# Splitting the weights ahead of the third q and k: another form of the shift, another order, and four or three pieces a slot

## The chip, the cores and the metric

The kernel runs on one core of one Trainium2 chip. The time is the device time of one execution in microseconds; before the change it is 1643.41 us, the median of three runs (1642.69 to 1644.14). The core has a matrix engine (TensorE, PE in the profile; PEld are its weight loads), a vector engine (VectorE, DVE), a scalar engine (ScalarE, ACT) and GpSimd (POOL). SyncE (SP) issues the transfers. Each engine works through its own list of instructions in order.

## The reference

Attention for 8 batches of 8 heads, 576 rows of 64, where each row keeps only its 32 largest scores; then a feed-forward block with a quick GELU over the 4608 rows of 512.

```python
scores = scale * np.matmul(q, k.transpose(0, 1, 3, 2))
kth = np.partition(scores, -top_k, axis=-1)[..., -top_k:-top_k + 1]
scores = np.where(scores >= kth, scores, -1000000000.0)
scores = scores - np.max(scores, axis=-1, keepdims=True)
attn = np.exp(scores)
attn = attn / (np.sum(attn, axis=-1, keepdims=True) + 1e-09)
attn_out = np.matmul(attn, v)
...
x = attn_out.transpose(0, 2, 1, 3).reshape(B * S, H * D)
h = x @ w_in
g = h * (1.0 / (1.0 + np.exp(-1.702 * h)))
out = g @ w_out
```

q, k and v are float32. The two weight matrices (512 x 2048 and 2048 x 512) come as 64-bit floats, since a float32 array is multiplied there by a 64-bit scalar.

## The kernel before

**Slots.** The attention is cut into slots. A slot takes one block of 128 rows of two heads (a head pair `hp`, four of them per batch) against all 576 keys; the last 64 rows of two head pairs share a slot. A batch has 18 slots. The function `slot(n)` writes out by hand the order of all engines' instructions for slots -1 to 9; `two_slots` does so for the rest, two at a time. The scheduler keeps this order, so an instruction that has to wait holds up what stands behind it on its engine.

**A slot's attention.** `scores(n + 2)` multiplies q and k on TensorE (L230) and ScalarE copies the result (`sc`, L237). `topk(n)` is VectorE's work: 14 instructions, eight that find the next eight maxima (L246) for one of the two heads and six that remove them (L249), numbered i = 0 to 13. In the next slot, `bounds` turns the smallest kept value and the largest into two numbers on GpSimd (`cut`, L265, and `low`, L266); `exponentials` does two passes on ScalarE (L274, L276) and sums up; `divide`, called at i = 5 of that slot's `topk`, takes the reciprocal on VectorE (L285, L287) and makes two diagonal matrices on GpSimd (`by`, L291). `turn` multiplies by them on TensorE, `values` multiplies by v.

**Loading and preparing.** The table `later`, filled by `at(n, ...)`, says in which slot what is loaded. q and k of the first and second head pair are loaded in slot -1, of the third in slot 0, of the fourth in slot 1. `prepare` transposes them on TensorE (L198, L204), and ScalarE copies them back (L200 to L207). All transfers go through SyncE in the order in which they are written.

**Weights.** They are cut into 32 pieces of 128 x 512, 512 KB each as they are loaded, and each is turned into 32-bit numbers of a kind of the kernel's own in these steps (`round_piece`), named as in the code: *size* on ScalarE (L144, from the high word), *shift* on VectorE (L145, three bits to the left), *low* and *sign* on ScalarE (L150, L149, in place in the raw buffer) and *finish* on GpSimd, an addition and a product (L140, L141). Raw pieces lie in 8 buffers, which come free with *finish*. The list `by_slot` says how many pieces are split in which slot: 2, 3, 4, 4, 4, 4, 3, 4 and 4 in slots 0 to 8. A slot's pieces are loaded one slot ahead; their shifts stand between VectorE's instructions of `topk` after i = 7, 8 and so on, one at each; their *finish* runs in the slot after, the first at i = 2 and the others after `divide`.

The shift is a scalar_tensor_tensor with a column of zeros, `none`, as its second input, spread over 512 columns.

**The feed-forward block** starts when 128 rows of all four head pairs are there, in slot 4 for the first time: `hidden` (L378), `tanh` (L395) on ScalarE, `gate` (L411) on VectorE up to slot 9, `project` (L426) from slot 7 on.

Of the kernel before, what the change touches and what calls it, by code (L numbers as in the profile page):

```python
# [9 lines left out]
ALU = mybir.AluOpType  # L10
ENG = mybir.EngineType
F32 = mybir.dt.float32
U32 = mybir.dt.uint32
# [3 lines left out]
P = 128  # L17
# [11 lines left out]
def kernel(  # L29
# [24 lines left out]
    nc = tc.nc  # L54
# [13 lines left out]
    PIECE = 512  # L68
# [12 lines left out]
    const = ctx.enter_context(tc.tile_pool(name="const", bufs=1))  # L81
# [20 lines left out]

    ident = const.tile([P, P], F32, name="ident")
    make_identity(nc, ident[:])
    none = const.tile([P, 1], U32, name="none")
    nc.vector.memset(none[:], 0)
    win = const.tile([P, CC, DFF], F32, name="win")
    wout = const.tile([P, FC, C], F32, name="wout")

# [14 lines left out]
    def round_piece(n):  # L124

        c, g = pieces[n]
        dst = wout[:, g, :] if c is None else win[:, c, g * PIECE : (g + 1) * PIECE]
        words = raw.pop(n)[:].rearrange("p (n w) -> p n w", w=2)
        low, high = words[:, :, 0], words[:, :, 1].bitcast(F32)
        bits, whole = dst.bitcast(U32), dst.bitcast(I32)

        def finish():
            nc.gpsimd.tensor_tensor(out=whole, in0=whole, in1=low.bitcast(I32), op=ALU.add)  # L140
            nc.gpsimd.tensor_tensor(out=dst, in0=dst, in1=high, op=ALU.mult)  # L141

        return {
            "size": lambda: nc.scalar.activation(dst, high, AF.Abs, scale=REBASE),  # L144
            "shift": lambda: nc.vector.scalar_tensor_tensor(  # L145
                out=bits, in0=bits, scalar=3, in1=none[:].to_broadcast([P, PIECE]),
                op0=ALU.logical_shift_left, op1=ALU.bitwise_or,
            ),
            "sign": lambda: nc.scalar.activation(high, high, AF.Sign),  # L149
            "low": lambda: nc.scalar.mul(out=low.bitcast(I32), in_=low, mul=2.0**-29),  # L150
            "finish": finish,
        }
# [37 lines left out]
    def prepare(name, b, hp):  # L190
        src = loaded.pop((name, b, hp))


        before = 0 if name == "q" else TAIL
        dst = qkt.tile([P, S + before], F32, name=f"{name}_t")
        full = ps_t.tile([P, 512], F32, name="tp")
        for t in range(NF):
            nc.tensor.transpose(full[:, t * P : (t + 1) * P], src[:, t, :, :], ident[:])  # L198
        scale = SCALE if name == "q" else 1.0
        nc.scalar.mul(out=dst[:, before : before + FULL], in_=full[:], mul=scale)  # L200
        (qT if name == "q" else kT)[b, hp] = dst
        if name == "k":
            ends = ps_t.tile([P, 512], F32, name="tp")
            nc.tensor.transpose(ends[:, 0:P], loaded.pop(("ends", b, hp))[:], ident[:])  # L204
            nc.scalar.mul(out=qT[b, hp][:, FULL:S], in_=ends[:, 0:TAIL], mul=SCALE)
            for to in (0, before + FULL):
                nc.scalar.copy(out=dst[:, to : to + TAIL], in_=ends[:, TAIL:P])  # L207
# [12 lines left out]
    def scores(n):  # L220
        b, t, hps = slots[n]
        ps = [ps_s.tile([P, 2, 512], F32, name="s_ps") for _ in range(2)]
        if t < NF:
            parts = [(i, 0, slice(0, P), slice(t * P, (t + 1) * P)) for i in range(2)]
        else:
            parts = [(i, p, slice(p * TAIL, (p + 1) * TAIL), slice(FULL, S)) for i, p in ((0, 0), (1, 1), (0, 1), (1, 0))]
        for c in range(2):
            for i, p, rows, cols in parts:
                on = slice(i * D, (i + 1) * D)
                nc.tensor.matmul(  # L230
                    ps[i][rows, c, 0:HALF],
                    lhsT=qT[b, hps[p]][on, cols],
                    rhs=kT[b, hps[p]][on, FIRST[i] + c * HALF : FIRST[i] + (c + 1) * HALF],
                )
        sc = st[n]["sc"] = scp.tile([P, 2, S], F32, name="sc")
        for i in range(2):
            nc.scalar.copy(out=sc[:, i, :].rearrange("p (c k) -> p c k", c=2), in_=ps[i][:, :, 0:HALF])  # L237
# [22 lines left out]
    def bounds(n):  # L260

        top = st[n]["top"]
        cut = st[n]["cut"] = small.tile([P, 2], F32, name="cut")
        low = st[n]["low"] = small.tile([P, 2], F32, name="low")
        nc.gpsimd.tensor_scalar(cut[:], top[:, :, TOPK - 1], -1.0, None, op0=ALU.mult)  # L265
        nc.gpsimd.tensor_tensor(out=low[:], in0=top[:, :, TOPK - 1], in1=top[:, :, 0], op=ALU.subtract)  # L266

    def exponentials(n):

        sc, cut, low = st[n]["sc"], st[n]["cut"], st[n]["low"]  # L270
        pr = st[n]["pr"] = prp.tile([P, 2 * S], F32, name="pr")
        den = st[n]["den"] = small.tile([P, 2], F32, name="den")
        for i in range(2):
            nc.scalar.activation(sc[:, i, :], sc[:, i, :], AF.Prelu, bias=cut[:, i : i + 1], alpha=HUGE)  # L274
        for i in range(2):
            nc.scalar.activation(  # L276
                pr[:, i * S : (i + 1) * S], sc[:, i, :], AF.Exp, bias=low[:, i : i + 1],
                accum_out=den[:, i : i + 1],
            )
# [37 lines left out]
    def turn_main(n):  # L317
        for i in range(2):
            turn(n, i * NF, MAIN[i], NF)

    def turn_ends(n):

        turn(n, 2 * NF, FULL, 1)
# [114 lines left out]
    def at(n, fn, *args):  # L438
        later.setdefault(n, []).append((fn, args))
# [4 lines left out]
    READY = (((-9, -8), (-7, -6), (-4, -3), (-2, -1)), ((-7, -6), (-4, -3), (-3, -2), (-1, -2)))  # L444
    FETCH = (((-13, -12), (-11, -10), (-7, -7), (-5, -4)), ((-11, -10), (-9, -8), (-5, -5), (-2, -2)))
    VALUES = ((-8, -7, 0, 0), (-8, -7, 2, 2))
    by_slot = dict(enumerate([2, 3, 4, 4, 4, 4, 3, 4, 4]))
    for n in by_slot:
        first = sum(map(len, list(by_slot.values())[:n]))
        by_slot[n] = list(range(first, first + by_slot[n]))  # L450
# [1 line left out]
    for hp in range(NP):  # L452
        for name in "qk":
            at(max(hp - 2, -1), load, name, 0, hp)
            at(max(hp - 2, -1), prepare, name, 0, hp)
    for hp in range(NP):
        at(hp - 1, load_v, 0, hp)
    for n in by_slot:
        for x in by_slot[n]:
            at(n - 1, load_piece, x)  # L460
    for b in range(1, B):
        for hp in range(NP):
# [3 lines left out]
            at(b * PER + VALUES[b % 2][hp], load_v, b, hp)  # L466
    unfinished = []

    def slot(n):
        todo = later.pop(n, [])  # L470
        for fn, args in todo:
            if fn is not prepare:
                fn(*args)
        preparing = [args for fn, args in todo if fn is prepare]
        settled = n > PROJECTS
        aside = SETTLED < n < N
        before = 0 <= n - 1 < N
        if before:
            bounds(n - 1)
            exponentials(n - 1)  # L480
        if n < 0:
            for m in range(2):
                for args in preparing:
                    if args[2] == m:
                        prepare(*args)
                scores(m)
        some = [round_piece(x) for x in by_slot.get(n, [])]
        for piece in some:
            piece["size"]()
        if 0 <= n and not settled:  # L490
            for args in preparing:
                prepare(*args)
            scores(n + 2)
        shifts = [piece["shift"] for piece in some]
        tanh(aside)
        for i, op in enumerate(topk(n) if 0 <= n < N else [lambda: None] * 14):
            op()
            if i == 2 and unfinished:
                unfinished.pop(0)()
            if i == 5:  # L500
                if before:
                    divide(n - 1)
                while unfinished:
                    unfinished.pop(0)()
            if i == 8 and not aside:
                gate(aside)
            if i > 6 and shifts:
                shifts.pop(0)()
        if aside:
            gate(aside)  # L510
        if settled:
            for args in preparing[:1]:
                prepare(*args)
        for piece in some[:2]:
            piece["low"]()
        going = settled and len(to_project) > (2 if n < N else 0)
        if going:
            project(range(G - 1))
        if before:
            turn_main(n - 1)  # L520
        if going:
            project(range(G - 1, G))
        if before:
            turn_ends(n - 1)
        for piece in some[2:]:
            piece["low"]()
        if before:
            values(n - 1)
        for piece in some:
            piece["sign"]()  # L530
            unfinished.append(piece["finish"])
        if settled and n + 2 < N:
            scores(n + 2)
        if settled:
            for args in preparing[1:]:
                prepare(*args)
        hidden()
# [106 lines left out]
```

## Time and profile before

| | value |
|---|---|
| time, median of 3 runs | 1643.41 us |
| profiled span | 1642.3 us |
| TensorE busy | 1578.7 us, 96% |
| VectorE busy | 1497.8 us, 91% |
| ScalarE busy | 1155.6 us, 70% |
| GpSimd busy | 756.2 us, 46% |
| TensorE in the first 130 us | 81.80 us |
| VectorE in the first 130 us | 113.69 us |

The slots are told apart by VectorE's first maximum over a fresh score tile (L246, `top<-sc`):

| slot | starts at, us | length, us | pieces split | pieces finished |
|---|---|---|---|---|
| 0 | 10.71 | 10.86 | 2 | 0 |
| 1 | 21.57 | 17.22 | 3 | 2 |
| 2 | 38.79 | 16.31 | 4 | 3 |
| 3 | 55.10 | 14.71 | 4 | 4 |
| 4 | 69.81 | 14.70 | 4 | 4 |
| 5 | 84.51 | 15.97 | 4 | 4 |
| 6 | 100.48 | 14.95 | 3 | 4 |
| 7 | 115.43 | 15.55 | 4 | 3 |
| 8 | 130.98 | 15.99 | 4 | 4 |
| 9 | 146.97 | 10.50 | 0 | 4 |

Shares of busy time over the whole span mix two stages, the first some 150 us, in which the weights are split, and the rest; they have to be read apart. In a timeline row the first number is the start and the second the duration[...]. A row with "x2" holds two instructions.

### The profile page before, as it was taken

What the parts mean: (1) busy time and instruction counts of PE and PEld (TensorE: products, weight loads), DVE (VectorE), ACT (ScalarE), POOL (GpSimd) and SP (SyncE); (2) the same over time, 40 slices, a digit from 0 to 9 for tenths busy, and PEclk for the clock granted to TensorE, in tenths of its full rate; (3) what the DMA queues carried; (4) which work ended last, traced back from release to release, by engine and by line L of the source; (5) the groups of instructions that cost most, each with busy time, mean ns of one, the idle gap of its engine ahead of it and who ended that gap; (6) DMA issues with size and microseconds to landing.
All of it is one profiled execution on the core that took longest, in us unless ns stands there. A gap on an engine that the chain in (4) does not pass through costs nothing.

```text
span 1642.3 us, 31956 instructions
## 1 busy us (share of the span) xinstructions
PE 1578.7 (96%) x11923; PEld 1179.0 (72%) x11923; DVE 1497.8 (91%) x3212; ACT 1155.6 (70%) x2449; POOL 756.2 (46%) x783
## 2 busy tenths in 40 slices
PE   5478899999999999999999999999999999999999
PEld 4466677777777777777777777777777777777776
DVE  6999999999999999999999998999999999999960
ACT  5886677777777777777777777677777777777761
POOL 2787444444444444444444444444444444444430
PEclk7789999999999999999999999999999999999999
DMA  8342101110001001101000100111000100000000
GB/s 215 116 142 62 29 22 29 29 43 16 22 15 43 22 22 29 30 22 37 8 21 9 43 22 22 30 29 44 15 22 15 43 22 22 22 8 8 7 8 14
DMA packets 125723, 56.59 MB, mean 34 GB/s; under 512 B 116864, under 2 KB 116864, under 8 KB 125568
## 3 DMA queue, kind: packets, MB, share of 16 engines
q1 hardware_dynamic: 125568, 54.55, 12.6%
q8 instruction: 94, 1.54, 0.4%
q14 instruction: 61, 0.50, 0.1%
HBM read 45.09 MB, written 9.44 MB: 33 GB/s over the span
## 4 chain that ended last, share of the span: by engine, by line
PE 88%; DVE 8%; ACT 2%; POOL 1%; issue 1%; DMA 0%; SPq 0%; POOLq 0%; ACTq 0%
PE ph L378 30%; PE po L426 29%; PE s_ps L230 10%; PE o L337 9%; PE tp L305 8%; DVE top L246 3%; DVE left L249 2%; PE tp L198 2%; DVE wout L145 1%; DVE win L145 1%; ACT sc L237 1%; DMA k_l<-in_k_dram 0%; ACT pr L276 0%; PE tp L204 0%; POOL wout L141 0%
## 5 line engine op out<-in xcount | busy, mean ns | idle before, releaser
L246 DVE MAX8 top<-left 128x8 f32<-128x576 f32 x864 | 610.1, 746 | 0.0
L426 PE MATMUL po<-wout,gT 128*128 128x512 f32 x1152 | 541.3, 593 | 0.0
L378 PEld LDWEIGHTS ph<-xT,win 128*128 128x128 f32 x4096 | 468.1, 192 | 41.8 <-issue 41.0
L378 PE MATMUL ph<-xT,win 128*128 128x128 f32 x4096 | 485.1, 277 | 0.0
L249 DVE MATCH_REPLACE8 left<-top,left 128x576 f32<-128x576 f32 x576 | 423.4, 742 | 0.0
L294 POOL TENSOR_SCALAR pr<-pr,rden 128x576 f32<-128x576 f32 x135 | 232.9, 1725 | 358.9 <-ACT th L395 354.9
L408 POOL TENSOR_SCALAR th<-th 128x512 f32<-128x512 f32 x133 | 198.7, 1494 | 224.2 <-ACT th L395 220.8
L274 ACT ACTIVATE sc<-sc,cut 128x576 f32<-128x576 f32 x288 | 208.1, 774 | 132.0 <-POOL cut L265 132.0
L315 ACT COPY pt<-tp 128x512 f32<-128x512 f32 (+1 forms) x432 | 193.2, 480 | 153.0 <-PE tp L305 142.5
L426 PEld LDWEIGHTS po<-wout,gT 128*128 128x128 f32 x1152 | 197.6, 191 | 142.0 <-issue 141.8
L237 ACT COPY sc<-s_ps 128x576 f32<-128x576 f32 x288 | 169.8, 643 | 78.4 <-PE s_ps L230 78.1
L305 PEld LDWEIGHTS tp<-ident,pr 128*128 128x128 f32 x1215 | 145.5, 141 | 108.7 <-issue 59.3
L276 ACT ACTIVATE pr<-sc,low 128x576 f32<-128x576 f32 x288 | 219.1, 764 | 0.0
L249 DVE MATCH_REPLACE8 left<-top,sc 128x576 f32<-128x576 f32 x288 | 211.5, 742 | 0.0
L246 DVE MAX8 top<-sc 128x8 f32<-128x576 f32 x288 | 201.9, 742 | 9.9 <-ACT sc L237 9.9
L230 PE MATMUL s_ps<-k_t,q_t 64*128 64x288 f32 (+1 forms) x1280 | 183.4, 433 | 1.3 <-ACT k_t L200 1.3
L305 PE MATMUL tp<-ident,pr 128*128 128x128 f32 x1215 | 177.2, 273 | 5.0 <-ACT pt L315 4.0
L409 POOL TENSOR_TENSOR gT<-th,h 128x512 f32<-128x512 f32 x133 | 169.6, 1275 | 11.1
L337 PE MATMUL o<-pt,v_l 128*64 128x128 f32 (+1 forms) x2560 | 160.8, 269 | 1.4 <-ACT pt L315 0.6
L337 PEld LDWEIGHTS o<-pt,v_l 128*64 128x64 f32 x2560 | 133.5, 139 | 31.6 <-ACT pt L315 16.1
L230 PEld LDWEIGHTS s_ps<-k_t,q_t 64*128 64x128 f32 (+1 forms) x1280 | 100.2, 178 | 60.2 <-issue 40.9
L265 POOL TENSOR_SCALAR cut<-top 128x2 f32<-128x2 f32 x144 | 32.2, 224 | 221.4 <-DVE top L246 217.3
(51 smaller groups left out, 1186.6 us busy)
## 6 DMA issues: line engine op xcount, KB each, us to landing
q_l<-in_q_dram SPq DMA_DIRECT2D x64, 128.0 KB, 2.6
k_l<-in_k_dram SPq DMA_DIRECT2D x64, 128.0 KB, 2.7
v_l<-in_v_dram SPq DMA_DIRECT2D x64, 128.0 KB, 2.6
raw<-in_moe_w_in_dram SPq DMA_DIRECT2D x16, 512.0 KB, 4.5
raw<-in_moe_w_out_dram SPq DMA_DIRECT2D x16, 512.0 KB, 3.6
out_dram<-ob SPq DMA_DIRECT2D x32, 256.0 KB, 2.1
ends<-in_q_dram SPq DMA_DIRECT2D x32, 32.0 KB, 2.3
ends<-in_k_dram SPq DMA_DIRECT2D x32, 32.0 KB, 2.4
```

Source lines behind the costliest of these rows:

```text
L230: nc.tensor.matmul(ps[i][rows, c, 0:HALF], lhsT=qT[b, hps[p]][on, cols], rhs=kT[b, hps[p]][on, FIRST[i] + c * HALF : FIRST[i] + (c + 1) * ...
L246: nc.vector.max(top[:, i, 8 * r : 8 * r + 8], (left if r else sc)[:, i, :])
L249: nc.vector.match_replace(left[:, i, :], top[:, i, 8 * r : 8 * r + 8], (left if r else sc)[:, i, :], LOWEST)
L274: nc.scalar.activation(sc[:, i, :], sc[:, i, :], AF.Prelu, bias=cut[:, i : i + 1], alpha=HUGE)
L276: nc.scalar.activation(pr[:, i * S : (i + 1) * S], sc[:, i, :], AF.Exp, bias=low[:, i : i + 1], accum_out=den[:, i : i + 1],)
L294: nc.gpsimd.tensor_scalar(pr[:, S : 2 * S], pr[:, S : 2 * S], rden[:, 1:2], None, op0=ALU.mult)
L305: nc.tensor.transpose(tp[:, c * P : (c + 1) * P], pr[:, at], ident[:])
L315: nc.scalar.copy(out=to, in_=tp[:, 0 : blocks * P])
L337: nc.tensor.matmul(o[j * D : (j + 1) * D, 0 : cols.stop - cols.start], lhsT=main[:, c, j, :] if c < NF else tail[:, j, :], rhs=pt[:, j * N ...
L378: nc.tensor.matmul(ph[:, i, :], lhsT=win[:, c, f * P : (f + 1) * P], rhs=xT[:, c, :], start=(c == 0), stop=(c == CC - 1),)
L408: nc.gpsimd.tensor_scalar(th[:], th[:], 1.0, None, op0=ALU.add)
L426: nc.tensor.matmul(po[:], lhsT=gT[:, i, :], rhs=wout[:, f, :], start=(f == 0), stop=(f == FC - 1))
```

## The change

Three things are changed. The shift becomes a tensor_scalar with one input, and the tile of zeros goes. Of slot 0's pieces the first two are loaded in slot -1 right after the first q and k; their *size* steps stand on ScalarE right after the copy of slot 0's scores, their *low* and *sign* at the start of slot 0, and their shifts at i = 1 and 2 of slot 0's `topk`. And the pieces are dealt out as 4, 3, 3, 4, 3, 4, 3, 4, 4. In slot 0, the preparation of the third q and k and the scores of slot 2 are written behind `topk`, after the *size* steps of pieces 2 and 3, whose shifts stand at i = 12 and 13. The purpose is to take work from VectorE in the opening stage and to use the start, when GpSimd has no pieces yet. What is computed stays the same.

```diff
--- before.py
+++ after.py
@@ -102,8 +102,6 @@
 
     ident = const.tile([P, P], F32, name="ident")
     make_identity(nc, ident[:])
-    none = const.tile([P, 1], U32, name="none")
-    nc.vector.memset(none[:], 0)
     win = const.tile([P, CC, DFF], F32, name="win")
     wout = const.tile([P, FC, C], F32, name="wout")
 
@@ -142,10 +140,7 @@
 
         return {
             "size": lambda: nc.scalar.activation(dst, high, AF.Abs, scale=REBASE),
-            "shift": lambda: nc.vector.scalar_tensor_tensor(
-                out=bits, in0=bits, scalar=3, in1=none[:].to_broadcast([P, PIECE]),
-                op0=ALU.logical_shift_left, op1=ALU.bitwise_or,
-            ),
+            "shift": lambda: nc.vector.tensor_scalar(bits, bits, 3, None, op0=ALU.logical_shift_left),
             "sign": lambda: nc.scalar.activation(high, high, AF.Sign),
             "low": lambda: nc.scalar.mul(out=low.bitcast(I32), in_=low, mul=2.0**-29),
             "finish": finish,
@@ -444,7 +439,7 @@
     READY = (((-9, -8), (-7, -6), (-4, -3), (-2, -1)), ((-7, -6), (-4, -3), (-3, -2), (-1, -2)))
     FETCH = (((-13, -12), (-11, -10), (-7, -7), (-5, -4)), ((-11, -10), (-9, -8), (-5, -5), (-2, -2)))
     VALUES = ((-8, -7, 0, 0), (-8, -7, 2, 2))
-    by_slot = dict(enumerate([2, 3, 4, 4, 4, 4, 3, 4, 4]))
+    by_slot = dict(enumerate([4, 3, 3, 4, 3, 4, 3, 4, 4]))
     for n in by_slot:
         first = sum(map(len, list(by_slot.values())[:n]))
         by_slot[n] = list(range(first, first + by_slot[n]))
@@ -453,10 +448,13 @@
         for name in "qk":
             at(max(hp - 2, -1), load, name, 0, hp)
             at(max(hp - 2, -1), prepare, name, 0, hp)
+        if hp == 0:
+            for x in by_slot[0][:2]:
+                at(-1, load_piece, x)
     for hp in range(NP):
         at(hp - 1, load_v, 0, hp)
     for n in by_slot:
-        for x in by_slot[n]:
+        for x in by_slot[n][0 if n else 2 :]:
             at(n - 1, load_piece, x)
     for b in range(1, B):
         for hp in range(NP):
@@ -466,7 +464,10 @@
             at(b * PER + VALUES[b % 2][hp], load_v, b, hp)
     unfinished = []
 
+    early = []
+
     def slot(n):
+        nonlocal early
         todo = later.pop(n, [])
         for fn, args in todo:
             if fn is not prepare:
@@ -484,13 +485,22 @@
                     if args[2] == m:
                         prepare(*args)
                 scores(m)
-        some = [round_piece(x) for x in by_slot.get(n, [])]
-        for piece in some:
+                if m == 0:
+                    early = [round_piece(x) for x in by_slot[0][:2]]
+                    for piece in early:
+                        piece["size"]()
+        some = early if n == 0 else []
+        some = some + [round_piece(x) for x in by_slot.get(n, [])[len(some) :]]
+        for piece in some[:2]:
+            for step in ("low", "sign") if n == 0 else ("size",):
+                piece[step]()
+        if 0 <= n and not settled:
+            if n > 0:
+                for args in preparing:
+                    prepare(*args)
+                scores(n + 2)
+        for piece in some[2:]:
             piece["size"]()
-        if 0 <= n and not settled:
-            for args in preparing:
-                prepare(*args)
-            scores(n + 2)
         shifts = [piece["shift"] for piece in some]
         tanh(aside)
         for i, op in enumerate(topk(n) if 0 <= n < N else [lambda: None] * 14):
@@ -504,14 +514,18 @@
                     unfinished.pop(0)()
             if i == 8 and not aside:
                 gate(aside)
-            if i > 6 and shifts:
+            if (i in (1, 2, 12, 13) if n == 0 else i > 6) and shifts:
                 shifts.pop(0)()
         if aside:
             gate(aside)
         if settled:
             for args in preparing[:1]:
                 prepare(*args)
-        for piece in some[:2]:
+        if n == 0:
+            for args in preparing:
+                prepare(*args)
+            scores(n + 2)
+        for piece in some[2 if n == 0 else 0 : 2]:
             piece["low"]()
         going = settled and len(to_project) > (2 if n < N else 0)
         if going:
@@ -526,8 +540,9 @@
             piece["low"]()
         if before:
             values(n - 1)
-        for piece in some:
-            piece["sign"]()
+        for i, piece in enumerate(some):
+            if n or i > 1:
+                piece["sign"]()
             unfinished.append(piece["finish"])
         if settled and n + 2 < N:
             scores(n + 2)
```

## The prediction

> **What bounds the kernel now.** I read first how busy each engine is in four long stretches of the span, then the same for the numbered slots of the opening stage. Columns: the stretch, its length, then the busy time of PE, PEld, DVE, ACT and POOL with instruction counts, the TensorE clock, the DMA share and GB/s.
>
> ```profile
> 0.00:130.00 130.00, 81.80 (x519) 64.67 (x520) 113.69 (x205) 97.77 (x198) 81.44 (x88) 0.76 0.53 157
> ...
> 300.00:600.00 300.00, 300.00 (x2221) 224.24 (x2220) 285.69 (x624) 217.52 (x461) 136.09 (x141) 1.00 0.11 26
> ```
>
> ```profile
> 21.57:38.79 17.22, 10.85 (x55) 7.71 (x56) 13.28 (x27) 13.23 (x28) 7.02 (x8) 0.57 1.01 298
> ...
> 55.10:69.81 14.71, 6.41 (x48) 5.33 (x48) 14.68 (x27) 12.27 (x24) 12.78 (x12) 0.77 0.31 106
> ```
>
> From 300 us on TensorE is never idle, so VectorE time there is worth nothing. Before about 157 us it is the other way round: in slot 3 (55.10 to 69.81) VectorE is busy 14.68 of 14.71 us and TensorE 6.41. All the weight work lies in this opening stage. TensorE's instruction list after slot 9 is not touched, so what the opening stage gains or loses should move the end by the same amount. The chain that ended last agrees: from slot 2 to slot 8 it runs nearly all on VectorE, L246, L249 and the shift of L145.
>
> Next, what a shift costs. The same line is seen free and in contention; columns are start, duration, instruction:
>
> ```profile
> 35.41 0.67 DVE L145 SCALAR_TENSOR_TENSOR win<-win,none 128x512 uint32<-128x512 uint32 x1
> ...
> 60.86 1.29 POOL L140 TENSOR_TENSOR win<-win,raw 128x512 int32<-128x512 int32 x1
> 60.90 1.80 DVE L145 SCALAR_TENSOR_TENSOR win<-win,none 128x512 uint32<-128x512 uint32 x1
> ...
> 62.23 1.63 POOL L141 TENSOR_TENSOR win<-win,raw 128x512 f32<-128x512 f32 x1
> ...
> 63.30 1.11 DVE L145 SCALAR_TENSOR_TENSOR win<-win,none 128x512 uint32<-128x512 uint32 x1
> 63.81 1.76 POOL L140 TENSOR_TENSOR win<-win,raw 128x512 int32<-128x512 int32 x1
> ```
>
> Alone it takes 0.67 us. Beside the two GpSimd steps of another piece it takes 1.80 or 1.11, and theirs grow from 1.29 to 1.63 or 1.76: they take turns. The shift begun at 60.90 ends at 62.70, which is 0.55 after L140's end at 62.15; L141, begun at 62.23, ends 1.16 after that 62.70. Summed by slot, the shifts are busy 1.36, 3.50, 5.09, 5.09, 5.07, 5.75, 4.67, 5.34 and 5.78 us in slots 0 to 8, together 41.66.
>
> Last, what holds slots 1 and 2, where VectorE does wait; start, length and link in the chain that ended last:
>
> ```profile
> 14.43 4.75 DMA k_l<-in_k_dram
> 19.31 1.10 PE tp L198 x4
> 20.43 0.61 ACT k_t L200
> 21.08 2.30 PE s_ps L230 x7
> 23.40 1.18 ACT sc L237 x2
> 24.58 1.11 ACT raw L150 x2
> 25.69 1.09 ACT raw L149 x2
> 26.79 0.71 ACT sc L274 x2
> ```
>
> The third k lands at 19.2. ScalarE, in order, must then copy k and the scores of slot 2 and do four weight steps before the exponentials of slot 0 (from 26.7, done at 29.6). VectorE waits for those 3.9 us in slot 1 and 1.5 us in slot 2.
>
> [...] The trace has no tensor_scalar of this size on VectorE, only 128x2[...] The free shift is followed by the next instruction 0.59 us after its start (35.41 to 36.00)[...]
>
> **The change, part by part.** *The form of the shift.* [...] I take 0.33, with the turn-taking kept. I work slot 3 out from the end of the reciprocal, at 0: two removals to 1.45; GpSimd's L140 holds until 2.6 (62.15 less 59.55), so shift 1 ends at 2.93; L141 runs its 1.16 to 4.06 while VectorE does a maximum (0.67) to 3.6 and waits; shift 2 to 4.4; L140 to 5.5, shift 3 to 5.85; L141 to 6.96, shift 4 to 7.3; two steps to 8.0 and two maxima to 9.36. Before it was 69.81 less 59.52, 10.3. So one slot with four shifts gains 0.9, since much of the saving is returned as waiting for GpSimd. With the gate (L411, 0.59 more) the same counting gives 10.2 for 11.5 in slot 5 (gain 1.25), 9.9 for 10.5 in slot 6 (0.6, three shifts), 10.2 for 11.1 in slot 7 (0.9) and 10.6 for 11.55 in slot 8 (0.95).
>
> *Four or three pieces a slot.* The list moves two pieces into slot 0 and takes one each from slots 2 and 4. A slot of three shifts ends at 5.85 + 2.77 = 8.6 after the reciprocal against 10.3, so slots 2 and 4 gain 1.7 each (their form included). In slot 0 GpSimd has no pieces, so four shifts cost 1.3, about what two cost now; its end, near 22, is not on the path because of the wait in slot 1.
>
> Do other engines allow it? ScalarE in slot 3 is busy 12.27 with four pieces; with 0.45 from the last maximum to the exponential's start this needs about 13.1, below the new 13.8. GpSimd with four pieces needs 8 x 1.25 + 1.2 + 0.4 + 1.1 of waiting for the reciprocal and about 1.2 for turns, 13.9, against 13.0 in slot 4, which gets four pieces to finish from slot 3: its next bound (L265) comes 0.5 to 0.9 late. VectorE asks for the exponential's sum only 4.1 us into a slot, and from L265's start the sum takes 3.2, so this is just hidden.
>
> *Two pieces ahead.* The loads of the first two go before the second q and k, and pieces 2 and 3 now stand ahead of the third. So at the third k, four pieces have gone over the queue instead of two. Each piece adds about 1.4 us (landings at 15.13 and 16.62; 23.46, 24.71 and 26.08), in part in place of DMA time that is now lost to issuing: until 11.8 us every small load lands 0.3 to 0.8 after the last, as they are issued, at 0.7 of the DMA engines. Adding up landings: first k 6.0; two pieces at 8.9 and 10.3 (4.5 after issue, as at 10.48 now); second q, k and first v in the 4.0 that such a group takes behind pieces (16.62 to 20.59), 14.3; two pieces to 18.4; third q and k 2.84 more, 21.2 against 19.5. On ScalarE the size steps of the early pieces and their low and sign (2.3) move ahead of the third k's copy, where it stood waiting for it, and pieces 2 and 3 take their old place. So the exponentials of slot 0 come later by what the k comes later: 1.7 us. With no loss at all it would be 0.5; with both pieces' full 2.8 and the moved ScalarE work partly exposed, 4.5. Behind that wait are the division of slot 0 on VectorE and all after it, so the 1.7 goes fully on the path. In slot 1 itself nothing is won: the next exponentials come 14.8 after these, as ScalarE's list between them is as before, and slot 2's wait stays.
>
> *The memset and the tile* (L105 and L106, 0.06 us before any data is there): nothing, hidden under the first loads.
>
> Sum: slot 2 1.7, slots 3 to 8 0.9 + 1.7 + 1.25 + 0.6 + 0.9 + 0.95 = 6.3, together 8.0; less 1.7: **6.3 us faster, 1637 us.**
>
> **Rivals.** (a) The new shift takes no turns with GpSimd: then even at 0.6 each a four-shift slot saves 2.35 and a three-shift slot 2.9 on VectorE, and GpSimd loses its 1.5 us of waits. ScalarE (13.1, 13.6 with a tanh) and GpSimd (13.1 where four pieces are finished) become the bound: slots 3 to 8 about 13.1 + 12.1 + 13.6 + 13.1 + 13.6 + 13.9 = 79.4 against 91.9; with slot 2's 2.9 and the 1.7 lost, 13.7 faster, 1630. For it: the rows of 0.67 show how much is waiting. [...] (b) [...] only the moved shifts gain, 2 x 1.04, less 1.7: 1643, no change. (c) The start is hurt more: 4.5 lost against the 2.1 of (b): 2.4 slower, 1646, and more if ScalarE makes VectorE wait for the third and fourth shift in slot 0 as well. For it: DMA is at 1.01 of its share in slot 1, with no room. Against: ScalarE now stands idle 1.85 us before the third q's copy and 0.68 before the k's, which the moved steps fill.
>
> **Chances.** Forecast 0.62, (a) 0.17, (b) 0.11, (c) 0.10. The range goes from (a) to just past (b), 1629 to 1644. Of the forecast's case about 0.08 falls within 0.2% (3.3 us), as a gain of 3 is inside its bounds: faster 0.72, same 0.19, slower 0.09.
>
> **What would show it.** Shifts of about 0.41 us alone in slot 0, and 0.6 to 1.5 in slots 3 to 8 with the GpSimd steps at 1.5 at most; 0.67 alone and 1.1 to 1.8 in contention, as now, would say (b); one length everywhere, beside GpSimd's steps too, would say (a). The first exponential of slot 0 near 28.4 instead of 26.7; near 31 would be (c). Slot 9 should start about 6 us before 146.97, and TensorE's time from there be unchanged; if the gain at slot 9 is larger than at the end, the sum's premise is wrong.

## The result, and the profile after

| | before | after |
|---|---|---|
| time, median | 1643.26 us | 1637.40 us |
| runs (four each) | 1642.69 to 1644.14 | 1636.0, 1636.73, 1638.08, 1638.66 |
| profiled span | 1642.3 us | 1634.2 us |

The ratio is 0.9964, with a 95% interval of 0.9946 to 0.9981: 3 to 9 us faster, 5.9 by the medians, where 6.3 were forecast. The two profiled spans differ by more, 8.1 us: each is of one execution, one of the longer ones of before (1644.08 us) and the shortest of after (1636.00). The lines that were shown of before have these counterparts. First the stretches and slots, with the same columns:

```profile
0.00:130.00 130.00, 85.02 (x538) 66.18 (x538) 111.64 (x217) 102.09 (x207) 78.64 (x92) 0.91 0.57 165
300.00:600.00 300.00, 300.00 (x2250) 224.07 (x2247) 285.74 (x622) 216.05 (x459) 136.56 (x142) 1.00 0.11 27
22.30:41.42 19.12, 13.37 (x64) 9.75 (x65) 13.39 (x26) 14.19 (x32) 12.11 (x12) 1.00 0.87 242
55.49:69.13 13.64, 6.60 (x50) 5.44 (x48) 13.61 (x27) 13.07 (x26) 9.53 (x10) 0.87 0.37 120
```

Slot 3 (the last row) is still VectorE's: 13.61 of 13.64 us, 1.07 less than before. Slot 1 (the third row) is longer, 19.12 for 17.22, and VectorE is busy in it for only 13.39. From 300 us on TensorE is busy throughout, as before. The clock column (third from the right) doesn't show a faster clock at the start, though the first row has 0.91 for 0.76: the eight score products begun at 22.73 take 2.50 us. In the kernel before, those at 21.08 took 2.50 too, at a recorded 0.50, and those at 12.81, at full clock, took 1.45. The trace of the changed kernel has no record of the clock before 40 us, and such a stretch counts as full.

The shifts of slot 3 and the GpSimd steps beside them:

```profile
59.77 0.17 DVE L282 RECIPROCAL rden<-some 128x2 f32<-128x2 f32 x1
61.25 1.30 POOL L138 TENSOR_TENSOR win<-win,raw 128x512 int32<-128x512 int32 x1
61.29 1.54 DVE L143 TENSOR_SCALAR win<-win 128x512 uint32<-128x512 uint32 x1
62.63 1.36 POOL L139 TENSOR_TENSOR win<-win,raw 128x512 f32<-128x512 f32 x1
63.43 0.85 DVE L143 TENSOR_SCALAR win<-win 128x512 uint32<-128x512 uint32 x1
63.96 1.47 POOL L138 TENSOR_TENSOR win<-win,raw 128x512 int32<-128x512 int32 x1
64.87 0.84 DVE L143 TENSOR_SCALAR wout<-wout 128x512 uint32<-128x512 uint32 x1
```

The waits are still there. The first shift, begun at 61.29, ends 0.28 after L138's end at 62.55; the second and third take twice what a shift takes alone, which is this (the shifts of slot 0, least, median and most ns):

```profile
L143 DVE TENSOR_SCALAR win<-win x4: 407/411/427, 11.9 to 22.0; 128x512 uint32<-128x512 uint32 x4
```

0.41 us for the former 0.67, a saving of 0.26. From a shift's start to the next instruction's it is 0.33 (11.88 to 12.21), for 0.59 before; this is the 0.33 that the prediction takes. The trace of before did not show it, as it has no instruction of this form and size.

The start, from the chain that ended last ("..." stands for lines left out):

```profile
14.13 5.31 DMA q_l<-in_q_dram
...
20.96 1.10 PE tp L193 x4
...
22.09 0.61 ACT k_t L195
...
22.73 2.30 PE s_ps L225 x7
...
25.05 1.18 ACT sc L232 x2
26.23 1.09 ACT raw L145 x2
27.33 1.08 ACT raw L144 x2
28.40 0.71 ACT sc L269 x2
```

From the transposition of the third k (20.96) on these are the same steps as before, each about 1.6 us later; the exponentials of slot 0 begin at 28.3 instead of 26.7. The chain enters by the third q here; the third k lands at 20.8 (its last load is issued at 16.1 and takes 4.7), for 19.2 before.

Where it adds up, by slot (start of the first maximum over fresh scores, and the slot's length, us):

| slot | start before | start after | difference | length before | length after |
|---|---|---|---|---|---|
| 1 | 21.57 | 22.30 | +0.73 | 17.22 | 19.12 |
| 2 | 38.79 | 41.42 | +2.63 | 16.31 | 14.07 |
| 3 | 55.10 | 55.49 | +0.39 | 14.71 | 13.64 |
| 4 | 69.81 | 69.13 | -0.68 | 14.70 | 12.92 |
| 5 | 84.51 | 82.05 | -2.46 | 15.97 | 14.75 |
| 6 | 100.48 | 96.80 | -3.68 | 14.95 | 14.17 |
| 7 | 115.43 | 110.97 | -4.46 | 15.55 | 14.53 |
| 8 | 130.98 | 125.50 | -5.48 | 15.99 | 14.91 |
| 9 | 146.97 | 140.41 | -6.56 | 10.50 | 10.50 |

Slots 9 to 14 keep the 6.56. Between slots 14 and 15 another 1.5 appears in these two traces, and from there to the end the difference stays at 8.05. No instruction differs there. TensorE's clock does; the rows are 6.8 us from the first half-clock moment, in the kernel before and in the changed one:

```profile
193.30:200.10 6.80, 6.36 (x45) 5.11 (x47) 6.77 (x17) 3.25 (x7) 1.92 (x3) 0.50 0.00 1
```

```profile
187.10:193.90 6.80, 6.72 (x59) 4.80 (x60) 6.77 (x17) 3.29 (x9) 2.11 (x3) 0.75 0.01 2
```

The granted clock is half for 6.8 us in one and for 3.4 in the other, 59 matmuls instead of 45 pass, and the 40 products with v take 2.64 us in the chain instead of 4.13. TensorE had stood idle for 4.0 us around the start of these rows in both. The half clock begins 0.47 before the idle time ends in the kernel before, and 0.12 before that in the changed one. Whether that moment sets its length is not shown: no run sets it by itself.

The start of slot 9 lies ahead of this, so it is the cleaner measure of the change and of the experiments. It too is read from one execution of each kernel: two experiments below whose instructions agree up to slot 7 (zeros in PSUM on the order of before, with and without held shifts) start that slot 0.5 us apart, so a difference of that size can't be read as an effect.

### The profile page after: what moved, and what is told of

The parts are those of the page before. It is cut to its first block, busy times and chain, and to the rows that moved or that the text cites. A ratio compares the mean times of both kernels' runs of the same rounds, so it can differ in the third digit from the quotient of the medians.

```text
span 1634.2 us, 31957 instructions
## 1 busy us (share of the span) xinstructions
PE 1576.2 (96%) x11923; PEld 1176.5 (72%) x11923; DVE 1489.5 (91%) x3211; ACT 1156.2 (71%) x2449; POOL 750.6 (46%) x783
## 3 DMA queue, kind: packets, MB, share of 16 engines
q8 instruction: 94, 1.54, 0.4%
## 4 chain that ended last, share of the span: by engine, by line
PE 88%; DVE 7%; ACT 2%; POOL 1%; issue 1%; DMA 1%; SPq 0%; POOLq 0%; ACTq 0%
PE ph L373 30%; PE po L421 29%; PE s_ps L225 9%; PE o L332 9%; PE tp L300 8%; DVE top L241 3%; DVE left L244 2%; PE tp L193 2%; DVE wout L143 1%; ACT sc L232 1%; DVE win L143 1%; ACT pr L271 0%; POOL wout L138 0%; POOL wout L139 0%; DMA q_l<-in_q_dram 0%
## 5 line engine op out<-in xcount | busy, mean ns | idle before, releaser
L260 POOL TENSOR_SCALAR cut<-top 128x2 f32<-128x2 f32 x144 | 32.5, 226 | 220.3 <-DVE top L241 220.3
```

## The experiments

The theory: the form of the shift brings the gain, less than its own time since shifts wait for GpSimd's steps; the order and the dealing bring about as much as the later third k takes. The rivals are put in each expectation. All times are medians; the ratio is to the kernel before.

**The form alone**

```diff
 # the kernel before
-            "shift": lambda: nc.vector.scalar_tensor_tensor(
-                out=bits, in0=bits, scalar=3, in1=none[:].to_broadcast([P, PIECE]),
-                op0=ALU.logical_shift_left, op1=ALU.bitwise_or,
-            ),
+            "shift": lambda: nc.vector.tensor_scalar(bits, bits, 3, None, op0=ALU.logical_shift_left),
```

> The kernel before with the shift's new form alone; loads, order and 2, 3, 4, 4, 4, 4, 3, 4, 4 pieces stay. Theory (the form brings the gain, and the new order and dealing about cancel, since the two moved shifts bring what the later third k takes): slot 2 gains 0.9, slots 3 to 8 0.9, 0.9, 1.2, 0.6, 0.9 and 0.95, so slot 9 starts about 6.4 us before the 146.97 of before, near 140.6, and the time is about 1637. Rival (the order and the dealing bring it, and the shorter shift is given back as waiting for GpSimd): slot 9 at 145 or later, time 1641 or more.

1638.31 us, ratio 0.9964 (0.9951 to 0.9976), slot 9 at 139.91, 7.06 earlier. This one line gives the whole gain of the change. At slot 9 its trace is even 0.5 ahead of the changed kernel's, which is within what two traces differ by, and the times can't tell the two apart. Its five executions took 1635.62 to 1639.66 us, a spread of 4.0; only the fastest was traced, so what sets them apart is not shown.

**The order and the dealing alone**

```diff
 # the changed kernel
-            "shift": lambda: nc.vector.tensor_scalar(bits, bits, 3, None, op0=ALU.logical_shift_left),
+            "shift": lambda: nc.vector.scalar_tensor_tensor(
+                out=bits, in0=bits, scalar=3, in1=none[:].to_broadcast([P, PIECE]),
+                op0=ALU.logical_shift_left, op1=ALU.bitwise_or,
+            ),
```

> The changed kernel with the old form of the shift (scalar_tensor_tensor with the column of zeros): the order and the dealing alone. Theory: the two shifts moved out of contention bring 2 x 1.04, the later exponentials of slots 0 and 1 take 2.2, so slot 9 starts within 1 us of 146.97 and the time is about 1643. Rival (order and dealing bring the gain): slot 9 near 141.5, time near 1638.

1643.86 us, ratio 1.0003 (0.9994 to 1.0011), slot 9 at 146.80, 0.16 earlier: no change. At the start of slot 2 this kernel is 2.42 behind, and slots 2 and 4 with a shift fewer each bring it back.

**The new dealing without the new order**

```diff
 # the kernel before, with the new form
-    by_slot = dict(enumerate([2, 3, 4, 4, 4, 4, 3, 4, 4]))
+    by_slot = dict(enumerate([4, 3, 3, 4, 3, 4, 3, 4, 4]))
```

> The kernel before with the new form and the dealing 4, 3, 3, 4, 3, 4, 3, 4, 4, but in the old order: all four pieces of slot 0 are loaded behind the first two q and k, their steps are written where they were. Theory: four pieces still go ahead of the third k, and all four low and sign pairs now stand behind it on ScalarE, so the exponentials of slot 0 come about 2.3 us later than in the changed kernel (28.3), near 30.6, and slot 9 starts near 142.7; time about 1639.5. Rival (loading two pieces ahead is worth nothing): slot 9 near 140.4, time near 1637.

1640.59 us, ratio 0.9981 (0.9974 to 0.9989), slot 9 at 143.72: 3.3 later than in the changed kernel, where about 2.3 were expected. The chain shows why, with four low and four sign steps where the changed kernel has two of each:

```profile
22.65 0.61 ACT k_t L195
...
25.62 1.18 ACT sc L232 x2
26.80 2.19 ACT raw L145 x4
28.99 2.19 ACT raw L144 x4
31.18 0.71 ACT sc L269 x2
```

The copy of the third k begins only 0.56 later than in the changed kernel, at 22.65, after ScalarE had stood idle for 0.80; the exponentials begin at 31.1 for 28.3. So loading and splitting two pieces ahead is worth 3.3 us once four pieces are dealt to slot 0, and makes up for a loss that only the dealing brings.

**GpSimd with half of its piece steps**

```diff
 # the changed kernel
         def finish():
-            nc.gpsimd.tensor_tensor(out=whole, in0=whole, in1=low.bitcast(I32), op=ALU.add)
             nc.gpsimd.tensor_tensor(out=dst, in0=dst, in1=high, op=ALU.mult)
```

> The changed kernel without the first of GpSimd's two steps per piece (the addition of the low words at L138), so the weights lack their last bits and GpSimd has half its work on them. Theory (VectorE waits its turn behind GpSimd in slots 2 to 8, and ScalarE is next, near 13.1 us a slot of four pieces and 12 of three): most shifts at 0.41 us, slots 3 to 8 together near 79 instead of 84.9, slot 9 near 134. Rival (turns cost little, slots are as long as VectorE's own work makes them): slot 9 at 139 or later.

This kernel leaves out the first of GpSimd's two steps for each piece, so its weights lack their last bits. 1625.51 us, a single run; slot 9 at 131.66. Slots 3 to 8 take 76.9 us together, even less than expected. Shifts in its slot 3:

```profile
61.27 0.42 DVE L142 TENSOR_SCALAR win<-win 128x512 uint32<-128x512 uint32 x1
62.28 0.85 DVE L142 TENSOR_SCALAR win<-win 128x512 uint32<-128x512 uint32 x1
63.72 0.85 DVE L142 TENSOR_SCALAR wout<-wout 128x512 uint32<-128x512 uint32 x1
65.22 0.41 DVE L142 TENSOR_SCALAR wout<-wout 128x512 uint32<-128x512 uint32 x1
```

Two of the four are no longer held up. This half of GpSimd's work on the pieces is worth 8.75 us to slot 9 (140.41 less 131.66), through these waits, through GpSimd itself coming late with the next bounds, or both. The next experiment takes the waits away and leaves GpSimd its work.

**Two inputs, the second in PSUM**

```diff
 # the changed kernel; n is the piece, 24 pieces in slots 0 to 6
+    none = ps_p.tile([P, C], U32, name="none", tag="po")
+    nc.vector.memset(none[:, 0:1], 0)
...
-            "shift": lambda: nc.vector.tensor_scalar(bits, bits, 3, None, op0=ALU.logical_shift_left),
+        def shift():
+            if n < sum([4, 3, 3, 4, 3, 4, 3]):
+                nc.vector.scalar_tensor_tensor(
+                    out=bits, in0=bits, scalar=3, in1=none[:, 0:1].to_broadcast([P, PIECE]),
+                    op0=ALU.logical_shift_left, op1=ALU.bitwise_or,
+                )
+            else:
+                nc.vector.tensor_scalar(bits, bits, 3, None, op0=ALU.logical_shift_left)
```

The bank is the one that `project` takes from slot 7 on, so slots 7 and 8 keep the new form.

> The changed kernel with the old scalar_tensor_tensor form for the 24 pieces of slots 0 to 6, but with its column of zeros in PSUM instead of SBUF: two inputs, one of them in SBUF. Theory [...]: every such shift near 0.67 us whatever GpSimd does, GpSimd's steps 1.29 in slots 2 to 6, ScalarE next near 13.1 us a slot of four; slot 9 starts near 136, time near 1633. Rival (VectorE and GpSimd take turns whatever the memory of the second input): shifts of 1.1 to 1.8 as in the kernel before, slot 9 near 145.

1631.73 us, ratio 0.9927 (0.9915 to 0.9940), slot 9 at 135.75. The groups (busy us and mean ns after the bar): the old form with its zeros in PSUM for the first 24 pieces, the new form with its turns for the last 8:

```profile
L145 DVE SCALAR_TENSOR_TENSOR win<-win,none 128x512 uint32<-128x512 uint32 x16 | 10.8, 674 | 2.1 <-ACT win L153 2.1
L150 DVE TENSOR_SCALAR wout<-wout 128x512 uint32<-128x512 uint32 x8 | 9.0, 1129 | 0.0
L145 DVE SCALAR_TENSOR_TENSOR wout<-wout,none 128x512 uint32<-128x512 uint32 x8 | 5.4, 673 | 0.0
```

In the kernel before, with the zeros in SBUF, the same instruction has these groups:

```profile
L145 DVE SCALAR_TENSOR_TENSOR wout<-wout,none 128x512 uint32<-128x512 uint32 x16 | 21.9, 1370 | 0.0
L145 DVE SCALAR_TENSOR_TENSOR win<-win,none 128x512 uint32<-128x512 uint32 x16 | 19.7, 1233 | 0.0
```

What took 1.2 to 1.4 us on average (1.19 and 1.35 with the new order and the zeros in SBUF) takes 0.67 with its zeros in the other memory, also where it begins 0.04 after a step of GpSimd, and GpSimd's steps in slot 3 stay at 1.29 to 1.31. Slot 3:

```profile
60.38 1.29 POOL L140 TENSOR_TENSOR win<-win,raw 128x512 int32<-128x512 int32 x1
60.42 0.68 DVE L145 SCALAR_TENSOR_TENSOR win<-win,none 128x512 uint32<-128x512 uint32 x1
61.69 0.67 DVE L145 SCALAR_TENSOR_TENSOR win<-win,none 128x512 uint32<-128x512 uint32 x1
61.74 1.30 POOL L141 TENSOR_TENSOR win<-win,raw 128x512 f32<-128x512 f32 x1
```

The instruction that is slower alone (0.67 for 0.41) beats the faster one here, since the two engines no longer take turns. The slots are then held elsewhere: slot 4 is down to 11.70 us, but slot 5 takes 14.87, because GpSimd, with four pieces to finish in slot 4, gives out the next bounds only at 80.58, 1.97 after slot 5's start, and VectorE waits 1.0 us for the sum of the exponentials and 0.7 for a tanh behind it.

**The same on the order of before**

```diff
 # the kernel before, with the zeros in PSUM as above for the 24 pieces of slots 0 to 6
```

> The kernel before (its loads, order and dealing), with the column of zeros in PSUM for the 25 pieces of slots 0 to 6 and the new form in slots 7 and 8. Theory: from the 139.9 of the form alone slots 2 to 6 gain 1.0, 0.6, 0.6, 1.1 and 1.0 until ScalarE bounds them; slot 9 near 135.6, time near 1633. Rival (turns remain): near 145.

1633.13 us, ratio 0.9935 (0.9922 to 0.9947), slot 9 at 134.79. (The pieces of slots 0 to 6 are 24 here too, not 25.) By its trace this is the better base by 1.0 us at slot 9. The time does not show it: the trace has half the clock for 3.4 us at 162.3, after which slot 12 takes 11.40 us for 9.91, and for 6.8 at 182.8, where the zeros in PSUM on the new order have 3.4; the mean granted clock of the two traced runs is 0.983 and 0.992.

**Shifts held over into the next slot**

```diff
 # the changed kernel
+        carried = held[:]
+        held.clear()
+        if 0 < n < 8:
+            held.extend(shifts[2:])
+            shifts = shifts[:2]
         tanh(aside)
+        if carried:
+            carried.pop(0)()
...
+            if i == 4 and carried:
+                carried.pop(0)()
             if i == 5:
```

> The changed kernel, but in slots 1 to 7 only the first two pieces' shifts stay behind the reciprocal; the third and fourth move into the next slot, one ahead of its first maximum and one at i = 4, when GpSimd has few or no piece steps. Theory (turns with GpSimd are what a shift costs beyond 0.4 us): a slot of four gains about 0.85, of three 0.44, slot 8 loses 0.66; slot 9 starts near 137.5 instead of 140.41, time about 1635. Rival (GpSimd with four pieces to finish is already the bound, and a later reciprocal delays it): slot 9 at 140 or later.

1633.76 us, ratio 0.9943 (0.9928 to 0.9958), slot 9 at 138.01. That is 2.4 earlier than in the changed kernel, half of it in slot 1 (17.92 for 19.12). Of the later slots it gains in 3, 5 and 7 (12.47 for 13.64, 14.09 for 14.75, 13.75 for 14.53) and loses in 4 and 6 (13.31 for 12.92, 14.36 for 14.17). In the first kind GpSimd finishes three pieces and in the second four, so with three the turns may be the cost and with four GpSimd's own work. But a slot of the first kind also has three shifts left for four, and one of the second four for three, so this run can't tell.

> The kernel before with the new form, and the third and fourth shifts of slots 1 to 7 moved into the next slot, ahead of its first maximum and at i = 4. Theory: as for the changed kernel with held shifts, about 0.85 a slot of four; slot 9 near 136.5, time near 1634. Rival (GpSimd is the bound with four pieces a slot): slot 9 near 139.5 to 140.

The same edit on the kernel before with the new form: 1635.81 us, ratio 0.9952 (0.9938 to 0.9966), slot 9 at 138.34. Only 1.6 ahead of the form alone, where 3.4 was expected. Here slots 3, 4 and 5 have four shifts and four pieces to finish in both kernels, and two of the shifts moved to a quieter place: 13.10 for 13.63, 13.74 for 13.63, 15.03 for 14.85, together 0.24 less. So where GpSimd finishes four pieces, as in five of slots 2 to 8, moving shifts brought next to nothing, as the rival had it. The gain is in slots 2 and 7 (15.13 for 16.35, 13.72 for 14.52), which have three shifts for four and three pieces to finish; which of the two counts there stays open.

**Both together**

```diff
 # the zeros in PSUM as above, and of the held shifts slot 7's alone
+        if n == 7:
+            held.extend(shifts[2:])
+            shifts = shifts[:2]
```

> The changed kernel with the zeros in PSUM for slots 0 to 6, and slot 7's third and fourth shifts moved into slot 8 (one ahead of the first maximum, one at i = 4). Theory: slots 7 and 8 are the only ones left in which shifts take turns with GpSimd; slot 7 falls from 15.07 to about 13.75 as with held shifts, slot 8 grows by 0.35; slot 9 near 134.8 instead of 135.75, time about 1631. Rival (GpSimd is the bound there): slot 9 at 135.7.

1632.27 us, ratio 0.9928 (0.9916 to 0.9941), slot 9 at 135.23; slot 7 takes 14.26 and slot 8 15.26. Half of what was expected.

> The same on the kernel before's loads, order and dealing: zeros in PSUM for slots 0 to 6, slot 7's third and fourth shifts in slot 8. Theory: slot 9 near 133.8 instead of 134.79; time 1632 if TensorE's half-clock windows between 160 and 190 us stay as they were with the zeros alone, 1630 if one of them goes. Rival: slot 9 at 134.8.

1632.04 us, ratio 0.9930 (0.9916 to 0.9944), slot 9 at 134.88, no earlier than its base. But this trace starts slot 7, up to which the instructions are the same, 0.5 later than the base's; slots 7 and 8 together take 0.4 less (14.28 and 15.28 for 15.07 and 14.91), much as in the run before (0.5 less). These two and the zeros in PSUM alone can't be told apart by their times; all three are about 5 to 6 us ahead of the changed kernel.

## Why the prediction was right

**The bound.** That VectorE holds the opening stage and TensorE all that follows, so that a gain there moves the end one for one, held: slot 9 starts 6.56 earlier (6.3 forecast), and so do slots 10 to 14; the medians differ by 5.9. The 1.5 that the two traces differ by after that (4.13 less 2.64 us for the 40 products with v) is the clock's, and no step of the prediction had it.

**The form of the shift.** The shift took 0.41 us alone, as the prediction has it, and the turns stayed (the rows of 1.54 and 0.85 above). That they would stay was the author's estimate: the trace of before shows them for the old form only. The working of slot 3, counted from the reciprocal, gave ends of the four shifts at 2.93, 4.4, 5.85 and 7.3, and 9.36 for the slot; counted from the reciprocal's end at 59.94, they ended at 2.89, 4.34, 5.77 and 7.21, and the slot at 9.19. Two slips in the working cancel: it lets GpSimd's step take 1.10 to 1.13 after a shift, though 1.16 had been read and came again, and ends a shift 0.33 to 0.35 after GpSimd's step, where 0.28 came. Gains by slot, forecast against measured: slot 3 0.9 and 1.07, slot 5 1.25 and 1.22, slot 6 0.6 and 0.78, slot 7 0.9 and 1.02, slot 8 0.95 and 1.08. Together slots 3 to 8 gained 6.95 for 6.3. Rival (b), a shift as long as before, is out by the 411 ns. Rival (a), no turns, is out by the rows of 1.54 and 0.85; with the second input in PSUM it could be made to happen, and slot 9 then came at 135.75, 11.2 before the 146.97, where (a) had counted 13.7.

**Four or three pieces.** Slot 4: 1.7 forecast, 1.78 measured. GpSimd's bounds came 0.9 late in slot 5 (L260 at 83.11, 1.06 after the slot's start, for 0.17 in slot 3), and VectorE did not wait for them, as worked out. Slots 1 and 2: slot 2 started 2.63 late where 1.7 was forecast, and gained 2.24 where 1.7 was; slot 3 started 0.39 late, where no delay was forecast.

**Two pieces ahead.** The third k landed 1.6 later and the exponentials of slot 0 began 1.6 later (1.7 forecast). That this comes from the dealing, and that the early pieces' steps only soften it, is shown by the dealing without the order (3.3 us worse), in which ScalarE waited 0.80 for the third k. In the changed kernel two lists end together: TensorE has the third k transposed at 22.06, and ScalarE is through with its early steps and the copy of the third q at 21.99. So the later k, to which the prediction puts the loss, is there only one of two causes: had it come earlier, ScalarE would still have begun its copy less than 0.1 earlier. Rival (c), 4.5 lost at the start, is out: VectorE did wait for a size step in slot 0, but for 0.67 only. A kernel with the third k ahead of pieces 2 and 3 was not tried.

**One step was missed.** In slots 1 to 6 the size steps of the third and later pieces also moved behind `scores(n + 2)`. In slot 1 the third shift waits 0.90 for it, and the exponentials of slot 1 come 2.2 us later than before, not 1.7: this may be most of the 0.4 by which slot 3 starts late. The prediction said that ScalarE's list in between was as before. That the sum came out so near is in part luck: what was lost here (0.4) and what the slots after gained beyond the working (0.65) have opposite signs.

**Net.** The prediction put 2.1 for the moved shifts against 1.7 lost; the experiment with the old form in the new order gives 0.16. The gain is the form's alone.

## What to carry to other kernels

When two engines take turns, ask of a faster instruction not only how long it is alone, but how long it is beside the other engine: here the form of 0.67 us alone, which stayed at 0.67 beside GpSimd with its zeros in PSUM, was worth 5 us more than the form of 0.41 alone, which took up to 1.55 beside GpSimd. A contended stage can be worked out turn by turn from one traced slot: here the gain of the new form came within 0.2 us a slot, while for shifts moved to another place, in the order of before, the forecast was 1.8 us out in all. Moving work ahead into an idle start can push back a later load, here the third k by 1.6 us; look for what stands behind the moved loads in their queue before counting the gain.

## What the hardware showed that was not expected

A scalar_tensor_tensor of 128 x 512 uint32 with one input in SBUF and one in PSUM took 673 to 674 ns on average beside busy GpSimd; with both in SBUF the same instruction took 1233 to 1370. The prediction had not thought of this; the run's own expectation had. A half clock of 6.8 us in the kernel before and of 3.4 in the changed one, around the end of the same 4.0 us of idle time on TensorE, makes 1.5 us of difference in the middle of the kernel between the traces of two programs whose instructions there are the same.
